# Softmax's scaling folded into the transposing product: twelve units of attention in a fused kernel

## The chip, the cores and the metric

The kernel runs on one core of a Trainium2 chip. The time is the device's, in microseconds (us), of one execution; lower is better. Five engines work side by side, each with its own queue of instructions in a fixed order: TensorE (PE, matrix products), VectorE (DVE), ScalarE (ACT), GpSimd (POOL) and SyncE (SP, which here only issues transfers). An instruction waits at the head of its queue until what it needs is done, and everything behind it waits too.

## The reference

Three layers follow one another; all inputs are fp32, the weights reach the kernel as 64-bit floats.

```python
# 1. attention: 4 batches x 8 heads, 512 local and 32 global tokens, window 32
s = q @ k.T / sqrt(64), masked;  e = exp(s - max(s))
a = e / (sum(e) + 1e-9);  out = a @ v
# 2. gated feed-forward (512 -> 1024 -> 512) with a convolution over 3 tokens
h = relu(x @ w_in);  out = (h * sigmoid(conv(h))) @ w_out
# 3. two-dimensional Fourier transform, layer norm, 512 -> 2048 -> 512
u = x + real(fft2(x));  out = u + relu(norm(u) @ w_ch1) @ w_ch2
```

Only the normalisation of `a` and the transpose of `a` ahead of `a @ v` are touched.

## The kernel before

Attention is cut into 32 units i, each two heads (h = 0, 1) by two blocks of 128 queries (a = 0, 1), with 224 keys for each block. A unit runs through these steps, named by the letters of the plan:

- `S`i: scores, PE, 4 products into two PSUM banks.
- `M`i.k (k = 0 to 3, one for each head and block): DVE adds the mask and takes the row's extreme, out of PSUM into the buffer `pb` (L337).
- `E`i.k: ACT, exponential in place in `pb`, with the row's sum (L347). `A`i adds 1e-9 (ACT), `R`i takes the four reciprocals (DVE, L355).
- `N`i.k: POOL multiplies `pb` by the reciprocal, 128 x 224 in place (L360).
- `T`i.h: PE transposes the half h, four 128 x 128 transposes by the identity (L376, L377) into one PSUM bank.
- `C`i.h: that bank is copied to SBUF, by DVE for h = 0 and by ACT for h = 1 (L383).
- `V`i: PE multiplies with the values, 8 products of 64 output rows by 128 columns, the two heads alternating.

Beside this run, in the same queues, the unpacking of 16 weights from 64-bit floats (`wa`, `wt` ACT; `wu` DVE, which does in place of `wt` for some weights; `wc` POOL; `ws`, `wo` DVE, L660 and L665; `wh` ACT; `wl` DVE, L677), and the first feed-forward tiles: `F`u on PE (12 products), `H`, `Y`, `TH`, `B` on ACT and DVE, `D`u.part on PE. `GS` to `GX` are the same as S to V for the global tokens.

The order of all this is written out by hand in `PLAN`, a list of these names; every engine executes its own names in the order of the list. The list reaches up to unit 12 and feed-forward tile 12. Units 13 to 31 come from a loop, and behind them the Fourier transform and the last layer; their order is set by the loop and by a scheduler's priorities.

Three pairs of `pb` buffers serve the units in turn; PSUM has eight banks, of which `s` and `t` (or `a0` to `a3` for odd units below 8) hold scores and transposes by turns.

Of the kernel before, what the change touches and what calls it, by code (L numbers as in the profile page):

```python
# [42 lines left out]
PLAN = """
lg lq0 lw0 lm1 lq1 li lv0 lw1 S0 lm0 lq2 lc lq3 wu0 wa0 lv1 M0.0 wc0 M0.1 E0.0 M0.2 E0.1 M0.3 S1 ws0 E0.2 E0.3 wo0 A0 lw2 R0 M1.0 wh0 N0.0 lw3 M1.1
E1.0 lq4 wl0 N0.1 E1.1 M1.2 N0.2 M1.3 T0.0 E1.2 E1.3 N0.3 C0.0 wa1 T0.1 wt1 wc1 A1 C0.1 S2 R1 ws1 N1.0 ca wo1 N1.1 V0 lq5 M2.0 wh1 N1.2 M2.1 E2.0 M2.2
wl1 N1.3 E2.1 T1.0 M2.3 E2.2 cd T1.1 E2.3 A2 S3 C1.1 C1.0 wa2 R2 N2.0 V1 wt2 M3.0 M3.1 E3.0 N2.1 M3.2 M3.3 E3.1 N2.2 wu3 lv2 T2.0 XH0 lq6 E3.2 N2.3
XL0 E3.3 C2.0 wc2 T2.1 A3 wa3 R3 S4 ws2 N3.0 C2.1 wo2 N3.1 V2 lw4 M4.0 wh2 N3.2 M4.1 lw5 E4.0 M4.2 N3.3 lw6 wl2 E4.1 T3.0 lw7 M4.3 E4.2 wc3 C3.0 T3.1
E4.3 A4 ws3 S5 C3.1 R4 wo3 wa4 N4.0 V3 M5.0 wh3 N4.1 M5.1 M5.2 E5.0 N4.2 M5.3 E5.1 T4.0 wl3 XH1 N4.3 wu4 E5.2 XL1 wc4 T4.1 E5.3 C4.0 A5 GS0.0 wa5 R5
GS0.1 ws4 C4.1 N5.0 wt5 lq7 GM0.0 N5.1 GM0.1 lv3 wa6 GK0 N5.2 lw8 S6 wo4 wt6 lq8 N5.3 wu7 GE0 V4 lw9 M6.0 wc5 GA0 M6.1 wh4 GR0 wc6 M6.2 E6.0 M6.3 T5.0
E6.1 GN0 wl4 E6.2 T5.1 C5.0 E6.3 F0 ws5 C5.1 wo5 A6 wa7 R6 wa8 ws6 wc7 GT0 wh5 wo6 N6.0 S7 GC0.0 GC0.1 N6.1 wl5 wh6 V5 H0 M7.0 N6.2 wt8 wl6 N6.3 E7.0  # L50
M7.1 F1 M7.2 XH2 wc8 M7.3 E7.1 ws7 E7.2 XL2 E7.3 T6.0 wo7 A7 H1 T6.1 Y0.0 C6.0 F2 wh7 R7 Y0.1 N7.0 C6.1 Y0.2 wa9 N7.1 wl7 GV0 TH0 N7.2 ws8 H2 GS1.0
wt9 N7.3 B0.0 GS1.1 GXH0 GM1.0 B0.1 wc9 GXL0 lq9 Y1.0 GM1.1 lv4 GK1 S8 B0.2 GE1 lw10 wo8 lw11 GA1 Y1.1 Y2.0 lw12 V6 wh8 GR1 lw13 M8.0 GN1 M8.1 lw14
E8.0 M8.2 lw15 F3 E8.1 M8.3 wl8 lq10 E8.2 lq11 E8.3 Y1.2 A8 Y2.1 TH1 T7.0 H3 R8 B1.0 N8.0 T7.1 wa10 C7.0 D0.0 N8.1 C7.1 Y2.2 B1.1 N8.2 D0.1 ws9 wt10
B1.2 N8.3 F4 wa11 wo9 wc10 wt11 wu12 wh9 wc11 ws10 GT1 H4 wl9 TH2 D1.0 GC1.0 GC1.1 B2.0 wa12 D1.1 wo10 B2.1 wc12 wa13 S9 ws11 wh10 wc13 B2.2 wo11 wt13
V7 Y3.0 M9.0 M9.1 E9.0 M9.2 F5 E9.1 M9.3 wl10 XH3 Y3.1 E9.2 E9.3 XL3 T8.0 A9 H5 Y3.2 T8.1 wh11 C8.0 D2.0 TH3 R9 C8.1 wl11 N9.0 D2.1 Y4.0 B3.0 N9.1
wa14 ws12 F6 B3.1 N9.2 wo12 wt14 N9.3 B3.2 wh12 ws13 GV1 wc14 H6 Y5.0 wl12 D3.0 lv5 GXH1 wo13 wa15 lq12 D3.1 GXL1 wc15 wh13 Y4.1 S10 Y4.2 wl13 TH4 V8
B4.0 lq13 M10.0 B4.1 M10.1 E10.0 M10.2 F7 E10.1 M10.3 B4.2 E10.2 Y5.1 E10.3 Y5.2 A10 Y6.0 T9.0 R10 ws14 N10.0 H7 T9.1 TH5 C9.0 N10.1 D4.0 C9.1 wo14
N10.2 D4.1 B5.0 wh14 N10.3 Y6.1 B5.1 F8 wl14 B5.2 Y6.2 Y7.0 D5.0 wu15 H8 TH6 Y7.1 D5.1 B6.0 Y7.2 S11 B6.1 ws15 TH7 B6.2 V9 M11.0 Y8.0 M11.1 E11.0
M11.2 M11.3 E11.1 F9 lv6 B7.0 XH4 lq14 Y8.1 E11.2 XL4 E11.3 T10.0 Y8.2 A11 H9 R11 T10.1 B7.1 wo15 N11.0 TH8 D6.0 C10.0 C10.1 N11.1 wh15 B7.2 D6.1
N11.2 B8.0 Y9.0 wl15 F10 B8.1 N11.3 B8.2 Y9.1 Y9.2 D7.0 H10 TH9 D7.1 Y10.0 B9.0 KA7.0 Y10.1 S12 B9.1 KB7.0 KA7.1 KC7.0 KB7.1 V10 M12.0 M12.1 E12.0  # L60
M12.2 E12.1 M12.3 F11 KC7.1 E12.2 B9.2 E12.3 Y10.2 A12 R12 TH10 T11.0 N12.0 H11 B10.0 T11.1 Y11.0 N12.1 C11.0 B10.1 D8.0 N12.2 C11.1 Y11.1 B10.2 D8.1
N12.3 Y11.2 F12 TH11 B11.0 B11.1 D9.0 B11.2 H12 Y12.0 D9.1 Y12.1 Y12.2
""".split()


# [1339 lines left out]
```

## Time and profile before

| | |
|---|---|
| median of 3 runs | 778.49 us (776.38 to 778.84) |
| the profiled execution | 780.79 us |
| its span, first to last instruction | 779.0 us |
| PE busy | 756.3 us (97%) |
| DVE busy | 557.4 us (72%) |
| ACT busy | 385.9 us (50%) |
| POOL busy | 157.7 us (20%) |
| granted clock of PE, mean over the span | 0.995 |

The shares are means over a kernel with very different stages: PE's lie near 100% from about 90 us on and lower before. A busy PE counts a matmul from its start to the end of its result, so that matmuls overlap and single durations add up to more than the time; what a block of them costs is read from the distance between starts, or from the chain of waits, which gives each its share of the path.

### The profile page before, as it was taken

Reading aid. Unit: us, or ns where it says so; the run is one execution under the profiler, and the core shown is the slowest. Engines: PE = TensorE matmul, PEld = TensorE weight load, DVE = VectorE, ACT = ScalarE, POOL = GpSimd, SP = SyncE. Lnnn points to the kernel's source line nnn. Section 1 sums busy time; section 2 is a strip of 40 time slices with the busy share of each in tenths; the row PEclk is TensorE's granted clock in tenths of the full one; section 3 lists DMA queues with packets and bytes.
Section 4 is the critical chain, followed back from the end, with each engine's and each line's share of the span. In section 5 each row is a group of like instructions: output and inputs, shape, how many; then the busy total and the mean of one; then the engine's idle time right before and its main releaser. Section 6 shows DMA issues by size and latency. Waiting matters only on the chain.

```text
span 779.0 us, 13835 instructions
## 1 busy us (share of the span) xinstructions
PE 756.3 (97%) x5224; PEld 695.4 (89%) x5224; DVE 557.4 (72%) x1274; ACT 385.9 (50%) x970; POOL 157.7 (20%) x228
## 2 busy tenths in 40 slices
PE   6798999999999999999999999999999999999998
...
GB/s 312 282 129 177 122 29 76 164 205 73 130 137 178 127 105 117 116 86 252 204 104 0 164 378 84 82 108 121 124 123 0 68 86 137 69 173 76 92 1 46
DMA packets 46594, 98.47 MB, mean 126 GB/s; under 512 B 5224, under 2 KB 26600, under 8 KB 46528
## 3 DMA queue, kind: packets, MB, share of 16 engines
...
q8 instruction: 41, 0.67, 0.3%
...
## 4 chain that ended last, share of the span: by engine, by line
PE 81%; DVE 9%; ACT 7%; DMA 2%; issue 1%; POOL 0%; SPq 0%; ACTq 0%
PE ps_a L170 29%; PE ps_g L170 20%; PE ps_pv L170 14%; PE ps_s L170 9%; PE ps_t L170 7%; ACT pb L347 3%; DVE y L562 2%; DVE pb L337 1%; DVE mag L660 1%; DMA raw_w<-in_w_out_dram 1%; DMA raw_w<-in_w_in_dram 1%; DVE w_w L677 1%; DVE mag L665 1%; DVE g L582 1%; ACT h L545 1%
## 5 line engine op out<-in xcount | busy, mean ns | idle before, releaser
L170 PE MATMUL ps_g<-x,w_w 128*128 128x256 f32 (+1 forms) x768 | 112.4, 296 | 2.3 <-DVE w_w L677 1.2
L170 PE MATMUL ps_a<-g,w_w 128*128 128x254 f32 (+1 forms) x768 | 113.5, 295 | 1.1 <-DVE g L582 0.6
L170 PEld LDWEIGHTS ps_g<-x,w_w 128*128 128x128 f32 x768 | 101.2, 190 | 8.9 <-issue 3.1
L170 PEld LDWEIGHTS ps_a<-g,w_w 128*128 128x128 f32 x768 | 101.1, 190 | 5.9 <-issue 3.8
L360 POOL TENSOR_SCALAR pb<-pb,sm 128x224 f32<-128x224 f32 x128 | 85.1, 681 | 81.5 <-DVE sm L355 72.6
L170 PE MATMUL ps_a<-hd,w_w 128*128 128x436 f32 (+1 forms) x384 | 81.6, 361 | 0.0
L562 DVE SCALAR_TENSOR_TENSOR y<-h,convw,y 128x254 f32<-128x254 f32 (+1 forms) x128 | 69.1, 541 | 16.3 <-ACT y L558 15.3
L170 PEld LDWEIGHTS ps_a<-hd,w_w 128*128 128x128 f32 x384 | 72.0, 188 | 4.5 <-DVE hd L1200 0.4
L347 ACT ACTIVATE pb<-pb,sm 128x224 f32<-128x224 f32 x128 | 60.4, 473 | 8.2 <-DVE sm L337 7.9
L192 POOL TENSOR_SCALAR mag<-mag 128x512 f32<-128x512 f32 x32 | 25.6, 800 | 178.8 <-ACT mag L191 178.5
L170 PE MATMUL ps_a<-hd,w_v 128*128 128x436 f32 (+1 forms) x288 | 61.0, 360 | 0.0
L170 PEld LDWEIGHTS ps_a<-hd,w_v 128*128 128x128 f32 x288 | 54.2, 188 | 3.0
L1199 ACT ACTIVATE hd<-hh 128x434 fp32r<-128x434 f32 x32 | 18.1, 568 | 59.5 <-DVE hh L1238 30.8
L170 PE MATMUL ps_s<-qk 64*128 64x224 f32 (+1 forms) x144 | 36.5, 406 | 6.9 <-DMA qk<-in_qk_dram 3.6
L567 ACT ACTIVATE y<-y 128x254 f32<-128x254 f32 (+1 forms) x64 | 27.4, 429 | 29.2 <-DVE y L562 29.1
L1200 DVE SCALAR_TENSOR_TENSOR hd<-hh,hd 128x434 fp32r<-128x434 f32 x32 | 19.4, 609 | 30.4 <-ACT hd L1199 30.4
L170 PE MATMUL ps_t<-qk 64*128 64x224 f32 (+1 forms) x144 | 36.3, 403 | 0.0
L227 ACT CAST w_w<-mag 128x512 fp32r<-128x512 f32 x20 | 12.4, 621 | 47.6 <-PE ps_t L170 11.7
L1015 ACT ACTIVATE hd<-ps_g 128x436 fp32r<-128x436 f32 x24 | 12.8, 533 | 46.5 <-PE ps_g L170 46.5
L582 DVE TENSOR_TENSOR g<-y,g 128x254 fp32r<-128x254 f32 (+1 forms) x64 | 28.5, 445 | 9.6 <-ACT g L580 9.6
L545 ACT ACTIVATE h<-ps_g 128x256 f32<-128x256 f32 (+1 forms) x64 | 25.2, 393 | 20.1 <-PE ps_g L170 20.1
L577 DVE SCALAR_TENSOR_TENSOR y<-y,h 128x254 f32<-128x254 f32 (+1 forms) x64 | 28.3, 442 | 9.5 <-ACT y L567 9.2
...
## 6 DMA issues: line engine op xcount, KB each, us to landing
...
```

The lines of the kernel that those rows point to most:

```text
L170: return pe.matmul(o, a, b, start=start, stop=stop)
L192: (clamp or dve).tensor_scalar(mag, mag, TOP, 2.0, op0=ALU.min, op1=ALU.max)
L347: last_exp[0] = act.activation(p, p, AF.Exp, bias=sm[:, k:k + 1], scale=-1.0, accum_out=sm[:, 4 + k:5 + k])
L360: gp.tensor_scalar(pb_of(i, k), pb_of(i, k), sm[:, 12 + k:13 + k], 1.0, op0=ALU.mult, op1=ALU.mult)
L545: act.activation(hbuf[u % NHB][:, h0:h0 + n], h_bank.pop(u), AF.Relu, scale=0.5)
L562: dve.scalar_tensor_tensor(y, o, convw2[:, m, x:x + 1], y, op0=ALU.mult, op1=ALU.add)
L567: act.activation(g_t[u], g_t[u], AF.Tanh, scale=0.5)
L577: dve.scalar_tensor_tensor(y, y, 1.0, hbuf[u % NHB][:, cc:cc + n], op0=ALU.add, op1=ALU.mult)
L582: dve.tensor_sub(gate[u][:, 1], y, f32(gate[u][:, 0]))
L1015: act.activation(hd[:, 0], o, AF.Relu)
L1199: act.activation(hd[:, 0], o, AF.Relu)
L1200: dve.scalar_tensor_tensor(hd[:, 1], o, 0.0, f32(hd[:, 0]), op0=ALU.max, op1=ALU.subtract)
```

## The change

In units 0 to 11 the scaling `N` goes. In its place a step builds, for each half of a unit, two 128 x 128 matrices with the reciprocals of the row sums on the diagonal: the identity multiplied by one scalar for each row. `Qp`i.h does that on POOL (21 halves), `Qa`i.h on ACT (the halves 1.1, 5.0 and 10.0). The transpose then is a true product: `pb`, unscaled, is the stationary operand, 64 columns at a time, and the diagonal matrix the moving one, so that what comes out is transposed and scaled at once. It takes 8 products for a half instead of 4 transposes. The matrices of two units are held in turn. Unit 12 and the loop behind it keep the old steps.

`PLAN` is written anew. PE's names stand in it in the same order as before, and the same weights are unpacked; the shift of the tail words is on DVE for weights 0, 2, 4 and 5 of the list (before: 0, 3, 4, 7, 12 and 15), and on ACT for the others.

```diff
     def micro():
+        diags = rb.tile([128, 2, 4, 128], F32, tag="r0", name="diags")
+
+        def diag(i, h, eng):
+            o, r = diags[:, i % 2, 2 * h:2 * h + 2], smalls[i][:, 12 + 2 * h:14 + 2 * h]
+            for k in range(2):
+                if eng is act:
+                    act.mul(o[:, k], ident, r[:, k:k + 1])
+                else:
+                    eng.tensor_scalar(o[:, k], ident, r[:, k:k + 1], 1.0, op0=ALU.mult, op1=ALU.mult)
+
+        def turn_scaled(i, h):
+            tb = t_bank[i, h] = bank((("a2", "a3") if solo(i + 1) else ("s", "t"))[h])
+            pb = pbs(i)[h]
+            for a in range(2):
+                for c in range(4):
+                    o = tb[64 * (c % 2):64 * (c % 2) + 64, 256 * (c // 2) + 128 * a:256 * (c // 2) + 128 * a + 128]
+                    mm(o, pb[:, a, 64 * c:64 * c + 64], diags[:, i % 2, 2 * h + a], True, True)
...
-            "T": lambda i, h: t_mm(i, ("a2", "a3") if solo(i + 1) else ("s", "t"), [h]),
+            "Qp": lambda i, h: diag(i, h, gp),
+            "Qa": lambda i, h: diag(i, h, act),
+            "Qd": lambda i, h: diag(i, h, dve),
+            "T": turn_scaled,
...
-E1.0 lq4 wl0 N0.1 E1.1 M1.2 N0.2 M1.3 T0.0 E1.2 E1.3 N0.3 C0.0 wa1 T0.1 wt1 wc1 A1 C0.1 S2 R1 ws1 N1.0 ca wo1 N1.1 V0 lq5 M2.0 wh1 N1.2 M2.1 E2.0 M2.2
+E1.0 M1.2 Qp0.1 T0.0 wl0 E1.1 E1.2 T0.1 C0.0 M1.3 C0.1 wa1 wt1 wc1 S2 E1.3 ws1 A1 V0 lw3 wo1 lq5 wa2 R1 M2.0 Qp1.0 M2.1 wh1 M2.2 wc2 Qa1.1 T1.0 M2.3
```

PE, the turn of unit 0 and the scores of unit 2 behind it. `ps_a2` and `ps_a3` are the banks of the two halves, `pb0` and `pb1` their exponentials, `ident` the identity. Before:

```order
L376 MATMUL ps_a2_194<-ident_85,pb0_90 128x128
L377 MATMUL ps_a2_194<-ident_85,pb0_90 128x128
L376 MATMUL ps_a2_194<-ident_85,pb0_90 128x128
L377 MATMUL ps_a2_194<-ident_85,pb0_90 128x128
L376 MATMUL ps_a3_205<-ident_85,pb1_91 128x128
L377 MATMUL ps_a3_205<-ident_85,pb1_91 128x128
L376 MATMUL ps_a3_205<-ident_85,pb1_91 128x128
L377 MATMUL ps_a3_205<-ident_85,pb1_91 128x128
L170 MATMUL ps_s_215<-qk_146 128x224
L170 MATMUL ps_t_216<-qk_146 128x224
```

After; x8 stands for eight products in a row:

```order
L169 MATMUL ps_a2_191<-diags_121,pb0_90 64x128 x8
L169 MATMUL ps_a3_203<-diags_121,pb1_91 64x128 x8
L169 MATMUL ps_s_220<-qk_147 128x224
L169 MATMUL ps_t_221<-qk_147 128x224
L169 MATMUL ps_s_220<-qk_147 128x224
L169 MATMUL ps_t_221<-qk_147 128x224
```

Four transposes of 128 x 128 for each half became eight products of 64 x 128 with the diagonal matrices as the moving operand; the scores of unit 2 (`ps_s`, `ps_t`) stand behind them as before.

ACT, the exponentials of unit 1 (`pb2`, `pb3`), the first two steps on weight 1 (`mag2`, `raw_w1`), the sum's 1e-9 (`sm`) and the copy of the second half of unit 0 (`pt1`). Before:

```order
L347 ACTIVATE pb2_92,sm_177<-pb2_92,sm_177 128x224 x2
L347 ACTIVATE pb3_93,sm_177<-pb3_93,sm_177 128x224 x2
L643 ACTIVATE mag2_121<-raw_w1_137 128x512
L651 ACTIVATE raw_w1_137<-raw_w1_137 128x512
L351 ACTIVATE sm_177<-sm_177 128x4
L383 COPY pt1_213<-ps_a3_205 128x512
```

After:

```order
L346 ACTIVATE pb2_92,sm_180<-pb2_92,sm_180 128x224 x2
L346 ACTIVATE pb3_93,sm_180<-pb3_93,sm_180 128x224
L382 COPY pt1_215<-ps_a3_203 128x512
L660 ACTIVATE mag2_122<-raw_w1_138 128x512
L668 ACTIVATE raw_w1_138<-raw_w1_138 128x512
L346 ACTIVATE pb3_93,sm_180<-pb3_93,sm_180 128x224
L350 ACTIVATE sm_180<-sm_180 128x4
L660 ACTIVATE mag_123<-raw_w8_149 128x512
```

The copy, which waits for PE, moved from behind the two weight steps and the sum to ahead of them, and one exponential of unit 1 moved behind them.

## Rows read from the trace of the kernel before

**Rows 1.** The page's part 2: busy tenths of PE in 40 slices
```profile
PE   6798999999999999999999999999999999999998
```

**Rows 2.** Table of stages: start:end, length, busy us of each engine, PEclk, DMA
```profile
17.50:34.50 17.00, 12.97 (x116) 9.00 (x116) 16.21 (x56) 16.15 (x49) 10.26 (x18) 1.00 0.67 236
34.50:41.50 7.00, 7.00 (x40) 6.09 (x39) 5.74 (x18) 5.45 (x18) 4.05 (x6) 0.51 0.76 295
41.50:51.30 9.80, 9.45 (x113) 7.70 (x111) 9.65 (x25) 9.09 (x27) 7.03 (x10) 1.00 0.00 1
51.30:63.20 11.90, 10.57 (x85) 9.12 (x85) 10.31 (x31) 9.72 (x28) 5.51 (x9) 1.00 0.95 351
63.20:75.70 12.50, 10.93 (x122) 9.58 (x122) 12.46 (x29) 11.13 (x30) 6.67 (x7) 1.00 0.16 53
75.70:86.20 10.50, 9.47 (x83) 8.42 (x82) 10.22 (x28) 6.93 (x21) 4.44 (x6) 1.00 0.38 149
86.20:95.30 9.10, 9.10 (x81) 8.53 (x80) 8.83 (x25) 7.15 (x22) 3.30 (x7) 1.00 0.52 182
95.30:104.90 9.60, 9.60 (x83) 8.97 (x82) 7.73 (x24) 6.92 (x22) 2.74 (x4) 1.00 0.01 2
```

**Rows 3.** Chain of waits, 95 to 105 us: start, length, what
```profile
95.39 0.38 PE ps_s L170
...
96.34 1.03 PE ps_pv L170 x16
...
99.19 0.11 PE ps_s L376
...
99.96 0.11 PE ps_t L377
...
103.30 1.62 PE ps_a L170 x12
104.92 0.38 PE ps_s L170
```

**Rows 4.** Timeline of PE, 11 to 17 us: start, length, instruction, count [idle before]
```profile
11.07 0.47 PE L376 MATMUL ps_a<-ident,pb 128*128 128x128 f32 x1 [0.88 <-POOL pb L360]
...
13.16 0.42 PE L377 MATMUL ps_a<-ident,pb 128*128 128x128 f32 x1
13.51 0.74 PE L170 MATMUL ps_s<-qk 64*128 64x224 f32 x1
...
15.31 1.97 PE L170 MATMUL ps_pv<-pt,v 128*64 128x128 f32 x16
```

**Rows 5.** Timeline of ACT, 12 to 15 us
```profile
12.49 0.47 ACT L347 ACTIVATE pb<-pb,sm 128x224 f32<-128x224 f32 x1
...
13.51 0.66 ACT L651 ACTIVATE raw_w<-raw_w 128x512 int32<-128x512 uint32 x1
...
14.16 0.57 ACT L383 COPY pt<-ps_a 128x512 f32<-128x512 f32 x1
```

**Rows 6.** Timeline of DVE, 14 to 16 us
```profile
14.29 0.18 DVE L355 RECIPROCAL sm<-sm 128x4 f32<-128x4 f32 x1 [0.83 <-ACT sm L351]
14.38 0.68 DVE L660 SCALAR_TENSOR_TENSOR mag<-mag,raw_w 128x512 int32<-128x512 int32 x1
...
15.84 0.38 DVE L337 CUSTOM_DVE_ANT_0 pb<-ps_s,mask 128x224 f32<-128x224 f32 x1
```

**Rows 7.** Single source lines, 0 to 100 us: count, duration ns min/median/max, first and last start
```profile
L360 POOL TENSOR_SCALAR pb<-pb,sm x48: 442/715/1399, 10.6 to 93.1; 128x224 f32<-128x224 f32 x48
...
L660 DVE SCALAR_TENSOR_TENSOR mag<-mag,raw_w x16: 650/682/1100, 8.9 to 86.5; 128x512 int32<-128x512 int32 x16
...
L655 DVE TENSOR_SCALAR raw_w<-raw_w x6: 416/429/834, 7.2 to 84.9; 128x512 int32<-128x512 int32 x6
```

**Rows 8.** Groups by line and shape, 0 to 101 us: count, busy us, mean ns
```profile
L647 POOL TENSOR_SCALAR mag<-mag 128x512 f32<-128x512 f32 x16 | 11.7, 736 | 13.0 <-ACT mag L643 12.2
...
L660 DVE SCALAR_TENSOR_TENSOR mag<-mag,raw_w 128x512 int32<-128x512 int32 x16 | 12.2, 762 | 0.0
```

More of the change, by code (lines that the diff above doesn't have):

```diff
@@ L43 @@
 PLAN = """
-lg lq0 lw0 lm1 lq1 li lv0 lw1 S0 lm0 lq2 lc lq3 wu0 wa0 lv1 M0.0 wc0 M0.1 E0.0 M0.2 E0.1 M0.3 S1 ws0 E0.2 E0.3 wo0 A0 lw2 R0 M1.0 wh0 N0.0 lw3 M1.1
-E1.0 lq4 wl0 N0.1 E1.1 M1.2 N0.2 M1.3 T0.0 E1.2 E1.3 N0.3 C0.0 wa1 T0.1 wt1 wc1 A1 C0.1 S2 R1 ws1 N1.0 ca wo1 N1.1 V0 lq5 M2.0 wh1 N1.2 M2.1 E2.0 M2.2
-wl1 N1.3 E2.1 T1.0 M2.3 E2.2 cd T1.1 E2.3 A2 S3 C1.1 C1.0 wa2 R2 N2.0 V1 wt2 M3.0 M3.1 E3.0 N2.1 M3.2 M3.3 E3.1 N2.2 wu3 lv2 T2.0 XH0 lq6 E3.2 N2.3
-XL0 E3.3 C2.0 wc2 T2.1 A3 wa3 R3 S4 ws2 N3.0 C2.1 wo2 N3.1 V2 lw4 M4.0 wh2 N3.2 M4.1 lw5 E4.0 M4.2 N3.3 lw6 wl2 E4.1 T3.0 lw7 M4.3 E4.2 wc3 C3.0 T3.1
@@ L48 @@
[L48 to L59, printed above, removed]
@@ L60 @@
-N11.2 B8.0 Y9.0 wl15 F10 B8.1 N11.3 B8.2 Y9.1 Y9.2 D7.0 H10 TH9 D7.1 Y10.0 B9.0 KA7.0 Y10.1 S12 B9.1 KB7.0 KA7.1 KC7.0 KB7.1 V10 M12.0 M12.1 E12.0
-M12.2 E12.1 M12.3 F11 KC7.1 E12.2 B9.2 E12.3 Y10.2 A12 R12 TH10 T11.0 N12.0 H11 B10.0 T11.1 Y11.0 N12.1 C11.0 B10.1 D8.0 N12.2 C11.1 Y11.1 B10.2 D8.1
-N12.3 Y11.2 F12 TH11 B11.0 B11.1 D9.0 B11.2 H12 Y12.0 D9.1 Y12.1 Y12.2
+lg lq0 lw0 lm1 lq1 li lv0 lw1 S0 lm0 lq2 lw2 lc wu0 wa0 lq3 M0.0 wc0 M0.1 lv1 E0.0 M0.2 E0.1 M0.3 S1 ws0 E0.2 E0.3 wo0 lq4 A0 R0 M1.0 wh0 Qp0.0 M1.1
@@ new lines @@
+E1.0 M1.2 Qp0.1 T0.0 wl0 E1.1 E1.2 T0.1 C0.0 M1.3 C0.1 wa1 wt1 wc1 S2 E1.3 ws1 A1 V0 lw3 wo1 lq5 wa2 R1 M2.0 Qp1.0 M2.1 wh1 M2.2 wc2 Qa1.1 T1.0 M2.3
+wl1 E2.0 T1.1 E2.1 C1.0 S3 C1.1 wu2 E2.2 ws2 V1 E2.3 M3.0 A2 ca M3.1 E3.0 lv2 R2 M3.2 Qp2.0 XH0 M3.3 lw4 wo2 E3.1 Qp2.1 lq6 T2.0 E3.2 XL0 T2.1 wh2
+C2.0 S4 E3.3 wl2 C2.1 A3 cd lw5 V2 wa3 lw6 wt3 wc3 R3 M4.0 M4.1 E4.0 Qp3.0 M4.2 E4.1 M4.3 Qp3.1 T3.0 ws3 E4.2 E4.3 T3.1 C3.0 A4 S5 wa4 R4 wo3 Qp4.0
+C3.1 wu4 Qp4.1 wh3 V3 M5.0 wa5 M5.1 wc4 wl3 E5.0 T4.0 wc5 M5.2 XH1 T4.1 C4.0 E5.1 GS0.0 XL1 C4.1 GS0.1 E5.2 GM0.0 lq7 wa6 GM0.1 GK0 lv3 S6 wt6 wc6
@@ new lines @@
+M5.3 lw7 wu5 GE0 lw8 ws4 V4 lq8 E5.3 M6.0 lw9 A5 M6.1 GA0 E6.0 R5 GR0 M6.2 Qp5.1 Qa5.0 M6.3 E6.1 wo4 GN0 T5.0 E6.2 T5.1 ws5 E6.3 F0 C5.0 C5.1 A6 wo5
+wh4 wa7 GT0 R6 wl4 Qp6.0 wh5 S7 ws6 Qp6.1 GC0.0 GC0.1 H0 wc7 wl5 V5 wt7 M7.0 Y0.0 M7.1 F1 E7.0 M7.2 M7.3 XH2 wo6 E7.1 XL2 E7.2 T6.0 E7.3 T6.1 Y0.1 A7
+C6.0 H1 C6.1 F2 R7 Y0.2 Qp7.0 wh6 ws7 TH0 Qp7.1 wa8 wl6 GV0 H2 B0.0 wc8 wt8 GS1.0 wo7 GXH0 GS1.1 B0.1 GM1.0 wh7 GXL0 lq9 GM1.1 Y1.0 lv4 GK1 S8 wa9
+lw10 B0.2 wl7 lw11 GE1 wc9 V6 lw12 M8.0 GA1 lw13 M8.1 wt9 GR1 M8.2 lw14 GN1 F3 E8.0 M8.3 lw15 Y1.1 E8.1 lq10 Y1.2 E8.2 lq11 ws8 E8.3 T7.0 A8 T7.1 H3
```

9 lines of the change are left out of this document (added).

## The prediction

> **What bounds the kernel now.** I read the page's slices first [rows 1]: PE, the matrix engine, is busy throughout from the fifth slice on and has its only holes in the first 90 us. Then the table of stages [rows 2], cut at the first score product of a unit: from 86.2 us on PE is busy for the whole of each stage, 9.1 and 9.6 us. Before that VectorE (DVE) is the full engine: 16.21 of 17.00 us, 10.31 of 11.90, 12.46 of 12.50, 10.22 of 10.50, with PE idle for 4.03, 1.33, 1.57 and 1.03 us in the same stretches. So two limits stand one after the other: up to about unit 10 the order on DVE (scores' minimum, weight unpacking, copies of P transposed) with ScalarE (ACT) interleaved, after it PE's work alone. The last is the chain of waits over one full stage [rows 3]: from one unit's scores at 95.39 to the next one's at 104.92 only PE stands in it. The hand-written order ends just there (its last product, D9, starts at 103.30). Behind it every engine has the same instructions in the same order in both kernels, so the question is only by how much the scores of unit 13, now at 104.92, move; what they move, the end moves too, since PE is full there.
>
> **The change on PE.** A unit's transposes are 8 instructions of 0.11 us (99.19 to 99.96) [rows 3], 0.88 us. In their place stand 16 products of 64 output rows by 128 columns. The trace of before has that shape in the product of P and V: 8 products in the order, 16 instructions in the trace, 1.03 us [rows 3]; that is 0.129 us a product, with the two 64-row halves alternating in the order exactly as in the new code. 16 products are 2.06 us: 1.18 us more for each unit, 14.2 us for twelve. The order on PE is otherwise unchanged, product for product. The bounds of a unit's 2.06 us: if nothing is shared between halves, 32 instructions by the 0.11 us of a full transpose, 3.5 us; from below 0.88 us.
>
> TensorE: Matmul & The Clock Gate (the Trainium skill), section Terms, speaks against the change: it calls the transpose mode of trn2 4 times faster for FP32. By that a unit would pay 4 x 0.88 us = 3.5 us, the upper bound; the row of P and V says 2.3 times, and the sum goes by the row.
>
> **The change on POOL and DVE.** 48 scalings of P on GpSimd (median 0.715 us, 34.3 us) go [rows 7]; 42 products with the identity, 128 columns instead of 224, come on POOL, 6 on ACT. Their price is not in the trace: 0.57 of the columns gives 0.41 us, no saving gives 0.715; I take 0.5, nearer to the first since columns are what shrinks, 21 us. Nobody waits long for POOL now, so this pays only through DVE, whose two-input operations lengthen while POOL works: the joins of L660 have a median of 0.682 us and a mean of 0.762 [rows 7, 8]. Three such operations per weight, 16 weights, 0.08 us: 3.8 us in all. POOL's scaling, 34.3 us beside 11.7 of clamps [rows 8], is some 0.7 of POOL's work there and falls by 0.4, so DVE gets 1.1 us back; bounds 0 and 3.8. Two shifts (L655, median 0.429 us [rows 7]) leave DVE for ACT, both in the stages from 51 us on: -0.9 us on DVE, and 2 x 0.55 us [rows 5] plus 6 diagonals of about 0.3 us (between nothing and the 0.47 us of an exponential) [rows 5] on ACT, 2.9 us together.
>
> **Where it lands, stretch by stretch.**
>
> Start (to 17 us): here the matmuls still run at half speed, PE's lower level (1.2 GHz): a product of P and V, at 15.31, 1.97 us for 1.03 [rows 3, 4]. So each half of the first unit costs 1.97 us: 11.07 + 3.9 = 15.0 us instead of 13.16 + 0.42 = 13.6. The ACT order puts the copy of the second half ahead of the next weight's two ACT steps, where it now stands behind them. So the copy starts at about 15.1 (now 14.16) [rows 5], the steps end at 15.1 + 0.5 + 2 x 0.55 + 0.1 = 16.8, and DVE's join, at 14.38 now [rows 6], waits for that: +2.4 us, with the next unit's minima (15.84) queued behind it on DVE. The scores of unit 2 (13.51) [rows 4] also slip by 1.4 us, but hide under the same wait. DVE waited 0.83 us just before [rows 6] for ACT, which is part of the same wait, and later waits of the next two units give a little back: I take **+2.0 us**, bounds 0 (the wait is absorbed) and +3.
>
> Middle (17.5 to 51 us): T1 to T4 add 4.7 us, into 4.03 us of idle PE; T5 falls in the stretch at the lower clock, 0.51 of full [rows 2], where PE has no hole at all, T6 in one with a hole of 0.35 us. The copy on DVE that waits for T5 and T6 will wait longer; DVE had 1.26 us of holes at 34.5 to 41.5. I charge 1.0 us of the 2.4, less half of the relief, 0.6: **+0.4 us**, bounds -2.5 and +3.
>
> From the scores of unit 8 to those of unit 11 (51.3 to 86.2): T7 to T9 add 3.5 us into 3.93 us of idle PE, so at most 0.4 us can be won however light DVE becomes, although it is 0.9 + 0.5 us lighter: **-0.4 us**, bounds -0.4 and +3.5 (holes and work at different places).
>
> From unit 11 to 13 PE has no hole: T10 and T11 are paid in full, **+2.4 us**, whatever happens before.
>
> Sum: 2.0 + 0.4 - 0.4 + 2.4 = **+4.4 us**. The profiled execution took 780.79 us (span 779.0), which becomes 785.2; it lies 2.3 us above the median of the runs, so for the median I add the same to 778.49: **782.9 us**. A difference of 0.3%, 2.3 us, is about what a measurement of this kernel can tell from none.
>
> **Rivals.**
>
> 1. Faster. The chain from reciprocal to transposed P gets shorter (two diagonals, then products, instead of four scalings of 0.715 us), and more products early keep PE at its upper clock through 34.5 to 41.5: the 7.0 us there hold 3.5 us of work. Then the start costs nothing, the middle gives 2.5 + 1.5 us of what the lower clock takes, and stages 8 to 11 their 0.4; with T10 and T11's 2.4 still paid, -2.0 us; with the whole 3.5 us of the clock and the full relief of DVE, -5: 773.5 us. It decides where DVE no longer waits for T5's copy. For it: PE's hole before 34.5 is what comes ahead of the fall. Against it: DVE is 95% busy before and after, and T5 itself grows there. Chance 0.14.
>
> TensorE: Matmul & The Clock Gate (the Trainium skill), section Part 4: PE-mode transpose, says that transposes do not count as work for the clock; true products in their place would then bring it up sooner. By that rule rival 1 becomes likelier. The trace neither shows nor excludes it: transposes here run at 0.11 us in a stretch of full clock, and the fall comes after a hole.
>
> 2. No change: all added products before unit 10 fit PE's holes, the start's wait is absorbed by the next units, and DVE's relief pays T10 and T11 but for 1 us: 779.5 us. Chance 0.19.
>
> 3. ACT becomes the limit: it has 11.13 us of work in the 12.50 us from unit 9 [rows 2], and 2.9 us more come in over the plan, with copies of P among its queue, for which PE and DVE wait. All 2.9 us on the path: +7.3, 785.8 us. Chance 0.12.
>
> 4. The halves do not run side by side: 2.6 us more for each unit instead of 1.18, which the holes cannot take: 12 x 2.6 = 31 less the 10 us of holes, some +20: 798 us. Against it: P and V has the same form. Chance 0.04. That the products are not made at all is excluded by the order.
>
> **Numbers.** Forecast 0.51, its own range 779.5 to 786.5, of which 0.07 falls within 0.3%. Slower by over 0.3%: 0.44 + 0.12 + 0.04 = 0.60. Within: 0.07 + 0.19 + 0.03 of rival 1 = 0.29. Faster: 0.11. The range leaves out the lower half of rival 1 and what lies beyond rival 3: 777 to 788.5 us.
>
> **What would show it.** In the profile of after: 32 instructions for a unit's turn, 2.06 us, where PE is full (right if between 2.0 and 2.2); the stages from 86 us on 10.3 and 10.7 us long instead of 9.1 and 9.6; DVE's first join after the copy of unit 0 at about 16.8 us and an ACT hole before that copy; POOL's work down by some 13 us; L660's mean nearer 0.68. Wrong if the scores of unit 8 come earlier than 51.3 us: then the order won more than the products cost, and the size of the start's term is the step that failed.

## The result and the profile after

The changed kernel takes 786.35 us (median of 4 runs, 785.34 to 788.04) where the kernel before takes 778.66: 1.0105 times as long, 95% interval 1.0092 to 1.0118. The profiled execution took 786.04 us, span 784.3, against 780.79 and 779.0. So the medians lie 7.7 us apart and the two profiles 5.3, since the profiled execution of before was itself 2.3 us above its median. Slower by over 0.3%, as forecast, and by more than the forecast 4.4 us.

The table of stages of after, cut at the first score product of units 2, 3, 5 (the last stretch before it), and so on: start:end, length, then busy us of PE, PE's weight loads, DVE, ACT and POOL, the granted clock of PE, the DMA share and GB/s. The counts stand in brackets behind the busy times. It answers [rows 2].

```profile
14.40:20.50 6.10, 4.10 (x59) 3.44 (x57) 4.11 (x14) 5.11 (x14) 1.95 (x4) 1.00 0.63 214
20.50:35.40 14.90, 13.21 (x179) 10.31 (x177) 12.68 (x47) 13.42 (x43) 8.11 (x15) 1.00 0.52 184
35.40:42.90 7.50, 6.58 (x73) 5.51 (x73) 6.90 (x24) 7.09 (x23) 3.95 (x6) 1.00 0.90 319
42.90:52.50 9.60, 9.58 (x130) 7.89 (x128) 8.28 (x24) 8.83 (x26) 6.34 (x9) 1.00 0.20 69
...
63.60:80.10 16.50, 13.06 (x145) 11.88 (x144) 14.41 (x34) 13.49 (x35) 6.04 (x8) 0.90 0.17 60
...
100.60:111.40 10.80, 10.80 (x105) 9.81 (x104) 8.23 (x26) 7.20 (x22) 1.74 (x4) 1.00 0.17 50
```

Two things are to be seen. The stretch at PE's lower clock that stood at 34.5 to 41.5 us [rows 2] is gone (1.00 in the rows at 20.5 to 42.9), and a new one lies in the stage of unit 9 (0.90). And DVE, nearly full before (12.46 of 12.50 in unit 9's stage [rows 2]), now idles for 2.1 us in that stage and for 2.0 in the first row.

From the starts of the score products in the two traces, the shift is taken apart like this (us, after less before):

| stretch | before | after | difference |
|---|---|---|---|
| start to unit 3 | 18.64 | 20.50 | +1.86 |
| unit 3 to 4 | 3.04 | 5.03 | +1.99 |
| 4 to 8 | 29.66 | 27.02 | -2.64 |
| 8 to 11 | 34.84 | 37.75 | +2.91 |
| 11 to 13 | 18.67 | 21.11 | +2.44 |

The sum, +6.56, is the shift of unit 13's scores (104.85 to 111.41). It stays within 0.3 us up to the end of the second layer. Single profiles differ by up to 2 us in the early stretches: kernel e9 of the experiments, which is the kernel before up to unit 10, has unit 8's scores at 49.39 us and unit 10's at 73.54, where the trace of before has them at 51.34 and 75.66. Part of that is the first loads: unit 1's scores start anywhere between 6.8 and 8.9 us in the traces. Counted from unit 1's scores, unit 3's come 2.1 us later in after than in before.

**The start.** DVE in after, 12 to 18 us (start, length, engine, line, operation, count, in brackets the idle time before and what ended it). It answers [rows 6].

```profile
12.76 0.69 DVE L382 COPY pt<-ps_a 128x512 f32<-128x512 f32 x1 [1.03 <-PE ps_a L169]
...
16.35 0.69 DVE L677 SCALAR_TENSOR_TENSOR mag<-mag,raw_w 128x512 int32<-128x512 int32 x1 [2.60 <-POOL mag L664]
...
17.77 0.36 DVE L336 CUSTOM_DVE_ANT_0 pb<-ps_s,mask 128x224 f32<-128x224 f32 x1
```

ACT's timeline in after at the same place, answering [rows 5]:

```profile
14.46 0.59 ACT L382 COPY pt<-ps_a 128x512 f32<-128x512 f32 x1 [2.39 <-PE ps_a L169]
14.95 0.67 ACT L660 ACTIVATE mag<-raw_w 128x512 f32<-128x512 f32 x1
```

The join of weight 1 starts at 16.35 (14.38 before), 2.60 us after DVE ran empty; ACT's copy (14.46) stands ahead of the weight's steps (the first at 14.95) and waited 2.39 us for the turn. Unit 2's minima move from 15.84 to 17.77.

**The stage of unit 9.** PE's timeline in after:

```profile
69.09 2.70 PE L169 MATMUL ps_g<-x,w_w 128*128 128x256 f32 x12 [3.44 <-DVE w_w L694]
71.73 1.60 PE L169 MATMUL ps_s<-diags,pb 128*64 128x128 f32 x16
73.16 1.04 PE L169 MATMUL ps_t<-diags,pb 128*64 128x128 f32 x16
...
75.67 1.63 PE L169 MATMUL ps_g<-x,w_w 128*128 128x256 f32 x12
...
80.15 0.45 PE L169 MATMUL ps_s<-qk 64*128 64x224 f32 x1
```

DVE's timeline in after, 62 to 74 us:

```profile
62.17 1.09 DVE L677 SCALAR_TENSOR_TENSOR mag<-mag,raw_w 128x512 int32<-128x512 int32 x1 [0.97 <-POOL mag L664]
...
65.49 0.68 DVE L694 TENSOR_TENSOR w_w<-mag,w_w 128x512 fp32r<-128x512 f32 x1
66.09 0.38 DVE L336 CUSTOM_DVE_ANT_0 pb<-ps_s,mask 128x224 f32<-128x224 f32 x1
...
67.76 0.68 DVE L420 TENSOR_TENSOR x<-ps_pv,x 128x512 fp32r<-128x512 f32 x1
68.36 1.28 DVE L694 TENSOR_TENSOR w_w<-mag,w_w 128x512 fp32r<-128x512 f32 x2
...
73.38 0.69 DVE L382 COPY pt<-ps_s 128x512 f32<-128x512 f32 x1 [2.02 <-PE ps_s L169]
```

F5 waits 3.44 us for the low part of its weight. On DVE that is the subtraction at 68.36, behind the low part of another weight (65.49), four minima (from 66.09), a gate product and an evacuation (67.76); the whole chain is late by the 0.97 us for which the join at 62.17 waited for POOL's clamp, which itself stood behind the diagonals of unit 8. Behind the hole the clock falls: F5 takes 2.70 us (1.63 for F6 at 75.67), half of unit 8's turn 1.60 (1.04 for the other). Late F5 makes the turn late, and DVE, next in order with the copy of it, idles 2.02 us at 73.38. From unit 9's scores to unit 10's it is 16.55 us, against 12.42 in before.

**The turn where PE is full**, PE's timeline in after, answering the transposes of [rows 3]:

```profile
104.45 1.09 PE L169 MATMUL ps_s<-diags,pb 128*64 128x128 f32 x16
105.38 1.04 PE L169 MATMUL ps_t<-diags,pb 128*64 128x128 f32 x16
```

### The profile page after: what moved, and what is told of

Its sections match the earlier page's. It is cut to its first block, busy times and chain, and to the rows that moved or that the text cites. A ratio compares the mean times of both kernels' runs of the same rounds, so it can differ in the third digit from the quotient of the medians.

```text
span 784.3 us, 14416 instructions
## 1 busy us (share of the span) xinstructions
PE 763.5 (97%) x5512; PEld 704.6 (90%) x5512; DVE 552.9 (70%) x1272; ACT 389.8 (50%) x978; POOL 146.6 (19%) x222
## 4 chain that ended last, share of the span: by engine, by line
PE 87%; ACT 5%; DVE 5%; issue 1%; POOL 1%; DMA 1%; SPq 0%; POOLq 0%; ACTq 0%; DVEq 0%
PE ps_a L169 31%; PE ps_g L169 22%; PE ps_pv L169 14%; PE ps_s L169 10%; PE ps_t L169 8%; ACT pb L346 2%; DVE y L561 1%; DMA mask<-in_mask_dram 1%; DVE pb L336 1%; POOL diags L635 1%; ACT pt L382 1%; ACT raw_r L193 0%; ACT mag L190 0%; ACT h L544 0%; DVE mag L677 0%
## 5 line engine op out<-in xcount | busy, mean ns | idle before, releaser
L359 POOL TENSOR_SCALAR pb<-pb,sm 128x224 f32<-128x224 f32 x80 | 50.9, 654 | 53.8 <-DVE sm L354 53.0
L191 POOL TENSOR_SCALAR mag<-mag 128x512 f32<-128x512 f32 x32 | 23.3, 727 | 177.9 <-ACT mag L190 177.7
L226 ACT CAST w_w<-mag 128x512 fp32r<-128x512 f32 x20 | 12.4, 621 | 44.3 <-PE ps_t L169 11.7
```

The costliest lines, as they stand in the source:

```text
L191: (clamp or dve).tensor_scalar(mag, mag, TOP, 2.0, op0=ALU.min, op1=ALU.max)
```

## The experiments

Every kernel was timed beside the kernel before. The order is "old" (that of the kernel before) or "new" (that of the changed kernel), the turn is "old" (scalings and transposes) or "new" (diagonals and products). The columns behind the ratio are from the profiled execution, in us: DVE's idle time between 10 and 90 us, and the times from unit 9's scores to unit 11's and from unit 11's to unit 13's.

| kernel | order | turn | ratio to before, 95% | DVE idle | 9 to 11 | 11 to 13 |
|---|---|---|---|---|---|---|
| before | old | old | 1 | 5.5 | 22.9 | 18.7 |
| after | new | new | 1.0105 (1.0092 to 1.0118) | 12.6 | 26.7 | 21.1 |
| e4 | old | new | 1.0003 (0.9994 to 1.0012) | 5.1 | 22.7 | 21.1 |
| e5 | new | old | 1.0084 (1.0069 to 1.0100) | 11.6 | 25.5 | 18.7 |
| e6 | new | new in 0-9 | 1.0067 (1.0054 to 1.0080) | 13.1 | 27.6 | 18.7 |
| e9 | old | new in 10, 11 | 1.0026 (1.0014 to 1.0038) | 4.4 | 23.1 | 21.1 |
| e8 | old | new in 0-9 | 0.9993 (0.9980 to 1.0006) | 4.6 | 22.8 | 18.7 |
| t4 | old | new in 4-9 | 0.9993 (0.9983 to 1.0003) | 6.1 | 22.7 | 18.7 |
| h2 | new to unit 4, then old | new | 1.0033 (1.0018 to 1.0048) | 6.2 | 22.7 | 21.1 |
| h1 | old to unit 4, then new | new | 1.0097 (1.0071 to 1.0122) | 13.0 | 28.0 | 21.1 |
| e1 | new, 1 move | new | 1.0065 (1.0051 to 1.0079) | 12.2 | 26.4 | 21.1 |
| t1 | new, 1 move | new | 1.0061 (1.0049 to 1.0074) | 10.1 | 26.7 | 21.1 |
| t3 | new, 5 moves | new | 1.0031 (1.0023 to 1.0040) | 7.7 | 24.0 | 21.1 |
| t5 | old, 3 shifts to ACT | new in 1-9 | 1.0000 (0.9988 to 1.0012) | 7.4 | 22.3 | 19.3 |

### Turn and order apart: e4, e5

The old order with the new turn (two pairs of diagonals where the first and third scaling stood; here for unit 0):

```diff
-N0.0 ... N0.1 ... N0.2 ... N0.3 ... T0.0
+Qp0.0 ... Qp0.1 ... T0.0
```

> The order of the kernel before, with the new turn: where the first and the third scaling of a unit stood on GpSimd, two diagonals stand each, and the turns are products. Theory O: the new order is what costs beyond the products themselves; here units 10 and 11 pay 2 x 1.2 = 2.4 us, the start about 1 us, the holes of TensorE take the rest: 781 to 783 us, unit 10's scores within 2 us of 75.66. Rival P: the products cost all of the 7.7 us in whatever order: 785 to 788. Third: the order was needed by the products (copies of P wait longer where they stood): above 788.

Measured: 779.11 us, ratio 1.0003. In the old order the new turn costs nothing that can be measured, less than theory O had it (781 to 783); unit 10's scores come at 72.12, 3.5 us ahead of before and 1.4 ahead of e9. The turn still costs 2.4 us from unit 11 to 13, and about as much comes back between units 4 and 9: 38.5 us, against 40.4 in e9 and 41.6 in before, which have the old turn there.

The new order with the old turn, here for unit 8:

```diff
-Qp8.0 ... Qp8.1
+N8.0 N8.1 ... N8.2 N8.3
```

> The new order, with the old turn: each pair of diagonals is replaced by the two scalings of P on GpSimd (those on ScalarE too), and the turns are transposes. Theory O: F5 still waits for its weight, so unit 9's stage stays about 3 to 4 us longer than before, units 10 and 11 cost nothing: 781 to 784 us, unit 10's scores at 78.5 to 80. Rival P: without the products the order costs nothing: 778 to 779.5, unit 10's scores at 75 to 76.

Measured: 784.82 us, ratio 1.0084, above the upper end of theory O's range. The order costs 0.8 to 1.0% with either turn. The hole before F5 belongs to the order too. PE's timeline at F5 in e5:

```profile
69.87 2.75 PE L170 MATMUL ps_g<-x,w_w 128*128 128x256 f32 x12 [3.52 <-DVE w_w L697]
```

The same in before:

```profile
65.23 1.69 PE L170 MATMUL ps_g<-x,w_w 128*128 128x256 f32 x12
```

The same in e4:

```profile
61.67 1.68 PE L169 MATMUL ps_g<-x,w_w 128*128 128x256 f32 x12
```

In the new order F5 waits 3.52 us with the old turn and 3.44 with the new one, and unit 9's scores to unit 10's take 16.54 and 16.55 us. In the old order F5 doesn't wait, and the same stretch takes 12.42 us (before) and 12.55 (e4).

The windows view of 10 to 90 us has, behind the length, PE, its weight loads and DVE. In after:

```profile
10.00:90.00 80.00, 71.14 (x821) 61.39 (x822) 67.36 (x201) 67.16 (x193) 35.67 (x55) 0.98 0.53 192
```

The same of e4:

```profile
10.00:90.00 80.00, 77.25 (x904) 66.67 (x902) 74.88 (x218) 70.18 (x202) 41.69 (x67) 1.00 0.56 205
```

The same of e5:

```profile
10.00:90.00 80.00, 68.92 (x590) 55.68 (x590) 68.39 (x196) 65.13 (x186) 41.38 (x60) 0.94 0.53 194
```

DVE gets 67.36 us of work done in these 80 us in after and 74.88 in e4: 7.5 us, and the medians differ by 7.2. That gave the theory of the later runs (V): DVE is the full engine up to unit 11, and what it idles there is paid at the end. In e5 PE's clock is part of the loss as well: its mean over these 80 us is 0.94, in e4 1.00.

### The price of the turn where PE is full: e6, e9

In e6 the changed kernel's units 10 and 11 are put back to scalings and transposes; in e9 the kernel before gets the new turn in these two alone.

```diff
 def turn_scaled(i, h):
+    if i in (10, 11, 12):
+        return t_mm(i, ("a2", "a3") if solo(i + 1) else ("s", "t"), [h])
```

> The changed kernel, with only units 10 and 11 put back to scalings and transposes. If the two turns are paid in full where TensorE is never idle: -2.4 us from 786.3 to 783.9 (783.4 to 784.4), the stages from unit 11 on 9.1 to 9.2 and 9.5 to 9.6 us instead of 10.34 and 10.76, and nothing before unit 10's scores differs. Rival: the scalings make the transposes wait instead, so that less than half of it comes back: 785 or more.

> The kernel before with the new turn in units 10 and 11 alone. Up to the scores of unit 10 it is the kernel before, so its trace is a second look at that stretch. Theory S: 778.4 + 2.4 = 780.8 us (780.3 to 781.5). Rival: the two diagonals take the place of four scalings of 0.7 us on GpSimd and the turns start earlier, so that less than 1 us is lost: 778.5 to 779.4.

Measured: 783.88 and 780.43 us. From unit 11 to 13 it is 18.67 to 18.69 us with the old turn and 21.09 to 21.11 with the new one in every kernel of the table but t5: 2.43 us for two units, whatever comes before. e9's total, +0.26%, is 2.0 us. What e6's expectation says of the time ahead of unit 10 did not come true in its profile: unit 9's stage takes 17.4 us there, for 16.55 in after.

### The low part of F5's weight: e1

`wl9` is the subtraction that F5 waits for.

```diff
-wl8 wh10 M9.0 wa12 M9.1 M9.2 XH3 wc12 M9.3 E9.0 B2.0 XL3 E9.1 E9.2 wl9
+wl8 wl9 wh10 M9.0 wa12 M9.1 M9.2 XH3 wc12 M9.3 E9.0 B2.0 XL3 E9.1 E9.2
```

> Only the subtraction that makes the low part of input weight 5 is moved: on VectorE it stands right behind that of output weight 2, ahead of the minima of unit 9, instead of four minima, one gate product and one evacuation later. Theory O (the loss of unit 9's stage is a matter of order: the product F5 waits for this low part): F5's hole of 3.44 us falls to about 1.1, VectorE's later wait of 2.02 us goes, unit 10's scores come at about 78.2 us instead of 80.15, and the time falls by 2.0 us (1.0 to 3.5) from 786.3. Rival P (the products' extra time on TensorE has to be paid somewhere once the holes are used): unit 10's scores stay within 0.6 us of 80.15 and so does the time. Rival G (the diagonals on GpSimd hold the clamps back, and VectorE's joins with them): the wait of 0.97 us before the join at 62.17 stays and only the later 2.02 us can go, at most -1.0.

Measured: 783.46 us; 1.0065 instead of 1.0105, some 3 us, inside theory O's range and outside the rivals'. But the profiled execution is the longest of its runs (785.88) and shows where the rest sits. PE's timeline in e1:

```profile
67.11 1.69 PE L169 MATMUL ps_g<-x,w_w 128*128 128x256 f32 x12 [1.18 <-DVE w_w L694]
...
74.14 2.91 PE L169 MATMUL ps_g<-x,w_w 128*128 128x256 f32 x12 [1.64 <-DVE w_w L694]
```

DVE's timeline in e1:

```profile
65.77 1.28 DVE L694 TENSOR_TENSOR w_w<-mag,w_w 128x512 fp32r<-128x512 f32 x2
...
71.48 0.68 DVE L382 COPY pt<-ps_s 128x512 f32<-128x512 f32 x1
...
72.98 1.10 DVE L694 TENSOR_TENSOR w_w<-mag,w_w 128x512 fp32r<-128x512 f32 x1
```

F5 comes 2.0 us earlier, DVE's copy no longer waits (71.48), and now F6 waits 1.64 us for the next weight's low part (72.98), in this execution with a fall of the clock behind it (2.91 us for F6). So the expected 78.2 us for unit 10's scores didn't come in this profile (80.14): one late weight was exchanged for the next. The other five executions took 782.87 to 783.69 us at a mean granted clock of 0.999 or 1.000 (0.998 in the profiled one), so most of the gain is theirs; no trace shows where in them it lies.

### The two halves of the order: h1, h2

Both take one order up to the scores of unit 4 and the rest of the names in the other order.

> The new turn throughout. Up to the scores of unit 4 the order of the kernel before (as in the run with the old order, its ScalarE shifts of weight 2 included), everything behind them in the new order. Theory S (the new order loses twice, 4.0 us before the first product F and 4.0 us at F5 and F6, and both reach the end): 786.3 - 4.0 = 782.3 us (781.5 to 783.5), the hole before F5 still over 2 us. Rival H (what the start loses is hidden under later waits, the loss at F5 and F6 counts alone): 785.5 or more.

> The other half: up to the scores of unit 4 the new order, everything behind them in the order of the kernel before; the new turn throughout. Theory S: 779.1 + 4.0 = 783.1 us (782 to 784), the order before F5 and F6 without a hole of more than 1.5 us. Rival H: 779.0 to 780.

Measured: 786.34 and 780.60 us; h1 as rival H has it, h2 between the two. If the two halves add up, h2 says that the new start costs 0.3%, 2.3 us, of the 3.2 us that its stretch from unit 2 to 4 loses against e4, and that the order behind unit 4 is the larger part. (Where its two orders meet, h2 also gets one shift of some 0.43 us more on DVE than e4 has.) h1 alone would say that the start is worth nothing, but it made a wait of its own at the seam. PE's timeline in h1:

```profile
26.84 1.09 PE L169 MATMUL ps_g<-pt,v 128*64 128x128 f32 x14 [2.29 <-ACT pt L382]
```

ACT's timeline in h1:

```profile
25.68 0.62 ACT L691 CAST w_w<-mag 128x512 fp32r<-128x512 f32 x1 [1.29 <-DVE mag L684]
26.21 0.58 ACT L382 COPY pt<-ps_a 128x512 f32<-128x512 f32 x1
```

The copy of unit 2 (26.21) stood behind a weight step that waited 1.29 us for DVE, and PE waited 2.29 us for the copy; behind that hole the granted clock was 0.80 and 0.77 in the two windows from 26 to 34 us. So such a cut is no clean test, and the single moves count for more.

### One copy moved at the start: t1

```diff
-E1.2 T0.1 C0.0 M1.3 C0.1 wa1 wt1 wc1 S2 E1.3 ws1 A1
+E1.2 T0.1 C0.0 M1.3 wa1 wt1 wc1 S2 E1.3 ws1 A1 C0.1
```

> The changed kernel with one item moved: on ScalarE the copy of the second half of unit 0's transposed P stands behind the two steps of weight 1 and unit 1's last exponential again, as in the kernel before, instead of ahead of them. Theory V (VectorE is the full engine up to unit 11, each microsecond that it idles there is a microsecond at the end; between 10 and 90 us it idles 12.6 us in the changed kernel and 5.2 us in the run with the old order): VectorE's wait of 2.60 us before the join at 16.35 goes, unit 2's minima start at about 15.3 instead of 17.77, and the time falls by 2 us, to 784.3 (783.5 to 785). Rival H (what is won at the start is lost again in later waits, as the run with the old start suggests): VectorE's idle time moves behind unit 4, 785.7 or more.

Measured: 783.97 us, ratio 1.0061 for 1.0105. The wait of 2.60 us is gone, unit 2 to 4 takes 9.00 us instead of 11.18, and the gain reaches the end, as theory V has it. The hole before F5 stays (3.45 us).

### Five moves: t3

The moves of e1 and t1, and:

```diff
-Qp8.0 ... wa11 wc10
+wc10 Qp8.0 ... wa11
-Y3.0 C8.0 wh11 D2.0 Y3.1 C8.1 D2.1 Y3.2 wa14 wl11
+wh11 Y3.0 C8.0 wl11 D2.0 Y3.1 C8.1 D2.1 Y3.2 wa14
```

> The changed kernel with that item moved and four more: the low parts of input weights 5 and 6 (VectorE) ahead of unit 9's minima and right behind unit 8's copy, the high part of the latter (ScalarE) one place earlier, the clamp of the eleventh weight (GpSimd) ahead of unit 8's diagonals. Theory V: against the run that moved the low part of input weight 5 alone (783.5) another 2.0 us at the start, 1.0 at the join that waited for the clamp, and about 1 at F6: 779.5 to 781 us, VectorE's idle time between 10 and 90 us at 6 to 8 us. Rival H: 783 or more.

Measured: 780.92 us, at the upper end of theory V's range. The windows view of 10 to 90 us in t1:

```profile
10.00:90.00 80.00, 73.86 (x854) 63.87 (x855) 69.89 (x208) 68.78 (x199) 34.23 (x54) 0.98 0.53 194
```

The same of t3:

```profile
10.00:90.00 80.00, 75.43 (x888) 64.80 (x890) 72.28 (x215) 70.84 (x207) 35.58 (x55) 1.00 0.56 203
```

PE's timeline in t3 at F5 and F6:

```profile
63.27 1.69 PE L169 MATMUL ps_g<-x,w_w 128*128 128x256 f32 x12 [0.65 <-DVE w_w L694]
...
68.97 1.69 PE L169 MATMUL ps_g<-x,w_w 128*128 128x256 f32 x12 [0.32 <-DVE w_w L694]
```

The holes before F5 and F6 are 0.65 and 0.32 us (3.44, and 1.64 in e1), the clock stays at 1.00, DVE's idle time is down by 4.9 us and the time by 5.4 (by the medians). The turn is the new one throughout: some 70% of the loss were five places in the order. The three moves that t3 has beyond e1 and t1 were not run one by one.

### Fewer units, less work on DVE: e8, t4, t5

> The old order with the new turn in units 0 to 9 alone; units 10 and 11 keep scalings and transposes. Theory S (early products fall into holes of TensorE and shorten the way to the transposed P; the last two are paid in full): 779.1 - 2.4 = 776.7 us (776 to 777.5), that is faster than the kernel before by 0.2%. Rival P (the ten turns cost as much as they give): 778 to 779.

> The order of the kernel before, with the new turn in units 4 to 9 alone. In the runs with the old order the stretch from unit 4's scores to unit 9's is 38.4 us with the new turn and 40.4 with the old one, while unit 0's turn costs 1.1 us (5.2 to 6.3 between the scores of units 1 and 2) and units 10 and 11 cost 2.4 us. Theory V: 778.3 - 1.5 = 776.8 us (776 to 777.5), faster than the kernel before by 0.1 to 0.3%. Rival (the gain in the middle hangs on the early units' turns too, or is the spread of single profiles): 778 to 779.

Measured: 777.94 and 778.22 us, both 0.9993: not to be told from the kernel before. Both miss the figure of their theory (S and V) by over 1 us, and t4 lies in its rival's range. From unit 4's scores to unit 9's t4 takes 41.3 us with the new turn there, e8 38.4: the gain in the middle isn't the new turn's by itself. The two differ in the turn of units 0 to 3, and in the clock. Windows of 4 us in before (the number ahead of the DMA share is the granted clock):

```profile
22.00:26.00 4.00, 2.76 (x28) 1.82 (x24) 3.96 (x12) 3.30 (x11) 2.48 (x6) 1.00 0.96 349
...
30.00:34.00 4.00, 2.07 (x14) 0.92 (x14) 4.00 (x9) 3.97 (x12) 2.19 (x4) 1.00 0.43 122
34.00:38.00 4.00, 4.00 (x26) 2.98 (x27) 3.56 (x15) 3.97 (x14) 3.82 (x6) 0.57 1.01 409
```

The same windows of t4:

```profile
22.00:26.00 4.00, 2.15 (x20) 1.46 (x20) 3.96 (x14) 3.30 (x11) 3.22 (x5) 1.00 1.01 387
...
30.00:34.00 4.00, 2.70 (x26) 1.72 (x22) 3.96 (x12) 3.97 (x11) 2.34 (x5) 1.00 0.41 112
34.00:38.00 4.00, 4.00 (x42) 3.84 (x42) 2.82 (x12) 3.25 (x12) 2.76 (x4) 0.57 1.01 399
```

The same windows of e8:

```profile
22.00:26.00 4.00, 3.45 (x40) 2.52 (x40) 3.97 (x14) 3.39 (x11) 2.90 (x5) 1.00 0.97 368
...
30.00:34.00 4.00, 2.77 (x34) 1.92 (x29) 3.97 (x12) 3.97 (x11) 1.65 (x5) 1.00 0.28 67
34.00:38.00 4.00, 4.00 (x57) 3.37 (x54) 4.00 (x14) 3.97 (x14) 3.18 (x4) 1.00 1.00 397
```

All six kernels with the old order agree: with the old turn in units 0 to 3 (before, t4; e9 too, 0.59) the clock is at its lower level for most of 34 to 38 us; with products there (e8; e4 too, and t5 from unit 1 on) it stays up. PE was busy 2.76 and 2.15 us of the four from 22 on in the first two, 3.45 in the third, and the hole at 30 to 34 is alike (2.70, 2.77 in t4 and e8).

TensorE: Matmul & The Clock Gate (the Trainium skill), section Part 4: PE-mode transpose, has it that transposes don't count as work for the clock. These rows agree with it, but do not single it out, since the products also fill time in which the transposes left PE idle. Nor is the turn all that counts: e5, with transposes throughout, is at 1.00 from 34 to 38 us and low at 18 to 22 (0.61) and 38 to 42 (0.67), and h1, with products, falls behind its hole at 26 us.

> The order of the kernel before, the new turn in units 1 to 9, and the shifts of the eighth, thirteenth and sixteenth weight (0.43 us each) on ScalarE instead of VectorE, behind the other ScalarE step of the same weight. Theory V (VectorE's work and idle time up to unit 11 set the end): against the run with the new turn in units 0 to 9 (777.9), 1.1 us less for unit 0's turn at the lower clock and 1.3 us less work on VectorE: 776.0 us (775.3 to 777.0), faster than the kernel before by 0.2 to 0.4%. Rival C (ScalarE, at 3.9 of 4 us busy in the stretches where I looked, becomes the limit): 777.5 or more. TensorE's granted clock stays at 1.00 from 30 to 46 us, as in the run with units 0 to 9, and doesn't fall to 0.57 as in the run with units 4 to 9.

```diff
-wt6 lq8 N5.3 wu7 ... A6 wa7
+wt6 lq8 ... A6 wa7 wt7
-wt11 wu12 wh9 ... B2.0 wa12
+wt11 wh9 ... B2.0 wa12 wt12
-wu15
+wt15
```

Measured: 777.91 us, ratio 1.0000: rival C's time, for another reason than a full ACT. The clock stayed at 1.00 from 30 to 46 us, as expected. ACT's timeline in t5:

```profile
55.91 0.68 ACT L662 ACTIVATE mag<-raw_w 128x512 f32<-128x512 f32 x1 [1.53 <-DMA raw_w<-in_w_out_dram]
```

DVE's timeline in t5:

```profile
57.40 0.42 DVE L581 TENSOR_TENSOR g<-y,g 128x254 fp32r<-128x254 f32 x1 [1.13 <-ACT g L579]
...
59.65 0.69 DVE L696 TENSOR_TENSOR w_w<-mag,w_w 128x512 fp32r<-128x512 f32 x1 [0.62 <-ACT w_w L691]
```

What DVE was spared became idle time (7.4 us for 4.6 in e8): ACT waits 1.53 us for a weight that the DMA has not yet delivered, and DVE waits 1.13 us for ACT. From unit 11 to 13 t5 takes 0.6 us longer than the other kernels with the old turn there, since a product waits for the last weight's low part. No version was found that beats the kernel before.

## Why the prediction was right, and where not

**Sign and size.** Slower was right, and 786.35 lies in the range. By the medians the forecast's +4.4 us was 3.3 short (7.7), by the profiles 0.9 (5.3). Against the shift of unit 13's scores, +6.56, it was 2.2 short: one term of four is wrong by 3.3 us, and the other three together came out 1.15 us smaller than forecast. That the median lies within the range is in part luck: it is 0.15 us below the upper end, and two of the four executions took longer than 786.5. And the sum laid more on PE than the runs do: in the old order the turn costs nothing measurable (e4), and the new order costs 0.84% even with the old turn (e5), so that most of the slowdown is the order's, of which the prediction priced only the start.

**PE, 1.18 us a unit: right.** It is 1.9 us from a turn's first product to the next block's (104.45 to 106.35), just below the 2.0 to 2.2 that the prediction asked for, and 1.22 us a unit more by the stages (10.34 and 10.76 us, forecast 10.3 and 10.7). The halves run side by side: in the trace two products start 0.007 us apart and the next pair 0.109 us later. Rival 4 is excluded. TensorE: Matmul & The Clock Gate (the Trainium skill), section Terms, calls the transpose mode 4 times faster for FP32. It doesn't say than what; as the ratio of these two turns the trace doesn't agree: by the starts of their products it is 1.90 us for 0.79 (99.03 to 99.82 in before), 2.4 times.

**Units 11 to 13, +2.4: right**, +2.44, and by e6 and e9.

**Start, +2.0: right.** Unit 3's scores come 1.86 us later. The join was forecast at 16.8 and came at 16.35, for the reason given, and t1, which moves that one copy, gives 2.4 us back (3.4 by the ratios). That it would reach the end (the upper part of the bounds, not the absorbed wait) holds too. The half speed at the start is seen in the durations alone (unit 0's turn takes 3.6 us, seven of the eleven later ones 1.9): the column of the granted clock says 1.00 from 10 to 18 us in both kernels.

**Middle, +0.4: right by its bounds, for two reasons that cancel.** Between units 3 and 4 it is +2.0: unit 2's turn did not find the idle PE that the term gave it, and PE waits 0.64 and 0.22 us for the diagonals. In the old order the same stretch takes 3.73 us with the new turn (e4) and 3.04 with the old one, so that some 0.7 of the 2.0 us are the products and 1.3 the order. Then units 4 to 8 take 2.6 us less, and the stretch at the lower clock is gone. That is the part of rival 1 that came true (PE stays at its upper clock); in the old order it goes with the 2 to 3 us between units 4 and 9 that pay for the products (e4, e8), and t4, where the clock falls, hasn't got them. Together -0.65, within -2.5 and +3.

**From unit 8 to 11, -0.4: the step that failed.** Measured +2.9 (unit 8's scores 1.2 late, unit 11's 4.1); unit 9's stage alone is 4.1 longer. The term compared PE's holes with PE's new work and took DVE as lighter; it didn't read where the new order puts the subtractions that F5 and F6 wait for. In its place the runs show that wait: 3.44 us before F5, and a stage of 16.5 us in the new order with either turn (after, e5), 12.4 to 12.6 in the old one (before, e4). The upper bound, +3.5, held, under the right name (holes and work at different places). The work did get lighter: DVE's whole time fell from 557.4 to 552.9 us. But in a stretch where DVE is the full engine it is its waits that count, and they grew by 7 us.

**Rivals 2 and 3.** The new turn in the old order (e4) gives rival 2's time: products in PE's holes, and the middle paying for units 10 and 11. That a lighter DVE pays, as rival 2 has it, isn't shown; t4 speaks for the clock. Rival 3's time (785.8) is nearer to the measured one than the forecast, but its reason isn't seen: in the stage of unit 9 ACT is busy for 13.49 of 16.50 us. Where ACT is the fullest engine (13.42 of 14.90 and 7.09 of 7.50 us in the rows from 20.50), the changed kernel loses nothing from unit 4 on.

**POOL, DVE.** The prediction's estimate for a diagonal was 0.5 us on POOL and 0.3 on ACT. These rows answer [rows 7, 8]. Line 635 of after by itself (count, min/median/max ns):

```profile
L635 POOL TENSOR_SCALAR diags<-ident,sm x42: 368/377/1319, 10.3 to 97.3; 128x128 f32<-128x128 f32 x42
```

Line 633 of after, the same view:

```profile
L633 ACT ACTIVATE diags<-ident,sm x6: 385/389/405, 18.3 to 86.6; 128x128 f32<-128x128 f32 x6
```

The groups by line in after (count, busy us, mean ns, idle before):

```profile
L635 POOL TENSOR_SCALAR diags<-ident,sm 128x128 f32<-128x128 f32 x42 | 24.4, 598 | 36.3 <-PE ps_t L169 18.9 <-DVE sm L354 12.5 <-PE ps_a L169 3.1
...
L677 DVE SCALAR_TENSOR_TENSOR mag<-mag,raw_w 128x512 int32<-128x512 int32 x16 | 11.7, 728 | 3.7 <-POOL mag L664 3.6
```

Median 0.377, mean 0.598 on POOL; 0.389 on ACT. The join's mean falls from 0.762 to 0.728, not to 0.68. POOL's work fell by 11.1 us (157.7 to 146.6) for the forecast 13.

**What stays open.** Between the second layer's last product and the last layer's first, after, e1, e4, h2, t1, t3 and t5 take 1.2 us less than before; e5, e6, e8, e9, h1 and t4 take at most 0.4 less. It is why the span grew by 5.3 us only. No run asked for the cause. Nor was the rest of the order's loss split up: t3 has the new turn as e4 has it, and is still 0.28% behind e4.
